# A fused RetNet and RWKV channel-mix kernel: v scaled on GpSimd in ten blocks, five differences moved, half-array transposes from block 3, and a new order of pieces

## The chip, the cores and the metric

The kernel runs on one core of a Trainium2 chip. The metric is the device time of one execution in microseconds. The core has five instruction queues that run side by side, each in its own order: TensorE (PE, with its weight loads PEld), VectorE (DVE), ScalarE (ACT), GpSimd (POOL) and SyncE (SP). SP, ACT and POOL issue DMAs. A wait is a semaphore ahead of an instruction; everything behind it in the same queue waits too.

## The reference

Two layers, one after the other, in float32. The first is a linear recurrence with a decay per head, the second a mixture of each token with the one before it, and two matrix products.

```python
# q, k, v: (B, H, S, D) = (4, 8, 768, 64)
for t in range(S):
    state = gamma[h] * state + outer(k[t], v[t])
    y[t]  = q[t] @ state / sqrt(D)
x = y.transpose(0, 2, 1, 3).reshape(B, S, 512)
x_prev = x shifted by one token, zero at each sequence's start
xk = mu_k * x + (1 - mu_k) * x_prev
xr = mu_r * x + (1 - mu_r) * x_prev
k2 = relu(xk @ w_k) ** 2            # w_k: 512 x 1024
out = sigmoid(xr @ w_r) * (k2 @ w_v)  # w_r: 512 x 512, w_v: 1024 x 512
```

## The kernel before

The 4 x 768 tokens are cut into twelve blocks of 256 tokens, three to a sequence. A block goes through two stages: attention in a chunked form, with a state carried between the blocks of a sequence, then the channel mix. There is no scheduler. The constant `ORDER` (lines 24 to 75) is a list of some 630 words; a loop at the end of the kernel reads them one by one and records the instructions of each, so the order of the words is the order in each engine's queue. A word is a piece, its block and its parts; `~v ~a ~p ~s` says which engine does it (VectorE, ScalarE, GpSimd, SP), and `@67` which PSUM banks it takes. So `vs.3~p` is block 3's scaling of v on GpSimd, and `K.0.2@1` is the key product of block 0, part 2, into bank 1.

The words, with the helper and its line in the kernel before:

- `lq lk lv` load q, k, v of a block (L232 in two halves of 64 columns a token, L237 in one); `wk wr wv` load weights (L725, L728, L732), always on POOL. Loads by POOL convert q and k to float16 on the way; those by SP do not, and `ck cq` convert after them (L245).
- `vs` scales v by powers of the decay (L255): 128x1024 float32 times a broadcast constant, result in float16.
- `Tq Tk` transpose q and k on TensorE. A "whole" block takes 16 matmuls over the full height of the array (L274); otherwise 32 matmuls of 64x64, on the two halves of the height (L280). `Eq Ek` copy the result out of PSUM (L243).
- `S` scores (L320, L333, L341), `M` their causal mask on VectorE (L349, L356), `C` the blocks' states (L368, L386, L397), `U` their running sum (L421), `G` its decay to the next block (L426 on ScalarE, L430 on VectorE), `I Y J` the products with the carried state and with the masked scores (L443, L464, L480, L491).
- `D` writes the result, times the factor gy, into the tile xT (L509, L516); `gy` builds that factor (L708 to L718).
- `dx` takes the difference of each token to the one before it (L531), `X.n.w.j` the mixture (L560): xk for w = 0, xr for w = 1, in four parts j. Both read two tiles in SBUF.
- `K` the key product (L574 for two blocks together, L584 for one), `Qa Qb` its ReLU and square on ScalarE (L593, L601, L605), `R` the gate product (L614), `s` its sigmoid (L620), `V` the value product (L626), `O` the product of both (L632), `st` the store on SP (L639). `Vc Oc sc` are the last 128 tokens in two column halves (L644, L651, L656).
- `z` is a filler: matmuls on zeros that nothing reads (L693 in float32, L700 in float16).

Blocks 3 and 4, 6 and 7, 9 and 10 share their K pieces. Raw loads of q, k and v go through rings of four tiles, the scaled v (`vs`) and the transposed q and k through rings of three. DMAs take their semaphores from two rings of eight, one for those issued by POOL and one for those issued by SP and ACT; each waits until the one eight places before it in its ring has landed.

What the change touches besides the order are the sets that choose the form of a block:

```python
WHOLE = (0, 1, 2, 3, 4, 5)     # L21
WIDE = (2, 3, 4)               # L22
def whole(n):                  # L208
    return n in WHOLE or n in WIDE
```

Of the kernel before, what the change touches and what calls it, by code (L numbers as in the profile page):

```python
# [36 lines left out]
R.1.1@7 X.2.0.1 vs.3~p M.3.0~v Ek.4~a K.2.3@1 Qa.2.3 K.2.0@6 Qa.2.0 M.3.1~v S.4.1@45 M.4.1~v
Tq.5@1 Eq.5~a C.3@23 U.3.0~v U.3.1 s.1.1 vs.4~v R.1.0@6 s.1.0 G.3~a K.2.1@0 I.3@45 Qb.2.3 S.4.0@23
M.4.0~v Y.3 C.4@67 U.4.0 U.4.1 G.4~a K.2.2@1 Qb.1.1 I.4@23 J.3 Qa.2.1 Qa.2.2 Y.4 Qb.2.0 D.3~v
V.0.0.0@6 Tq.6@45 J.4 dx.3~v V.1.1.0@7 D.4~v dx.4~v X.3.0.1 V.0.1.0@0 V.1.0.0@1 X.2.1.2 Qb.2.2  # L40
wv.1~p V.0.0.1 Eq.6~a V.0.1.1 lq.7~p lk.6~p Tk.6@45 Ek.6~a O.0.0 Tq.7@23 Eq.7~a V.1.0.1 S.6@45
lk.5~p Tk.5@6 X.3.0.2 X.3.0.3 X.3.0.0 K.3.3@2 Qb.2.1 K.3.2@3 O.1.0 Ek.5~a O.0.1 X.3.1.1 M.6~v
lv.5~p vs.5~v K.3.5@0 Qa.3.5 Qa.3.3 K.3.4@6 V.1.1.1 Qa.3.2 lv.6~p C.5@01 S.5@45 Qa.3.4 vs.6~v
C.6@23 Qb.3.3 Qb.3.2 O.1.1 M.5~v U.5.0 X.2.1.3 U.5.1 U.6.0~a U.6.1 U.6.2 U.5.2 U.6.3 K.3.0@6
X.2.1.1 Qa.3.0 Qb.3.0 V.2.0.0@7 K.3.6@4 Qa.3.6 K.3.7@6 st.0.1 Qa.3.7 Qb.3.7 I.5@01 I.6@45 V.2.0.1
K.3.1@3 Qa.3.1 Qb.3.1 X.2.1.0 R.2.0@6 lk.8~p Tk.8@23 lv.7~p Y.5 X.3.1.0 vs.7~v X.3.1.3 Y.6 X.3.1.2
s.2.0 R.3.1@6 D.5~v dx.5~v st.1.1 st.0.0 Ek.8~a X.5.0.3 O.2.0 X.5.0.0 V.2.1.0@2 X.5.0.1 R.3.0@3
D.6~v G.6~a Qb.3.4 s.3.0 s.3.1 lv.8~p R.2.1@0 s.2.1 X.5.1.3 X.5.0.2 R.4.0@1 s.4.0 V.2.1.1 lk.7~p
# [30 lines left out]
def kernel(  # L79
# [180 lines left out]
    def turned(n, a, j0):  # L260
        if whole(n):
            return banks("T", n, a, j0).bitcast(F16).rearrange("c (j i p) -> c j i p", j=NJ, i=2)
        pt = banks("T", n, a, j0).bitcast(F16)[:, :, 0 : 2 * NJ * D]
        return pt.rearrange("c u (j i p) -> c u j i p", j=NJ, i=2)

    def trans(a):
        def go(e, n, j0=0, j1=NJ):
            pt = turned(n, a, j0)
            src = (K16 if a else Q16)(n)
            for j in range(j0, j1):  # L270
                for i in range(2):
                    if whole(n):
                        for s, h, jo, hp in heads(j):
                            nc.tensor.transpose(  # L274
                                pt[low(s), j, i, :], src[:, h, i * D : i * D + D], ident
                            )
                        continue
                    for u in range(2):
                        for s, h, jo, hp in heads(j):
                            nc.tensor.transpose(  # L280
                                pt[low(s), u, j, i, :], src[low(u), h, i * D : i * D + D],
                                ident[low(u), low(u)],
                            )
# [506 lines left out]
```

## Time and profile before

| What | Value |
|---|---|
| Median of 3 runs | 156.21 us (155.82 to 156.54) |
| Span of the profiled execution, first to last instruction | 154.9 us |
| TensorE busy | 146.0 us, 2423 matmuls |
| VectorE busy | 126.9 us, 205 instructions |
| ScalarE busy | 99.4 us |
| GpSimd busy (DMA issues included) | 55.5 us, 65 instructions |
| DMA | 22.31 MB in 45768 packets |
| HBM read, written | 24.31 MB, 6.29 MB |

The span is one profiled execution; its time in the manner of the runs is not listed, and the median of the runs stands 1.3 us above the span. Busy shares of TensorE are not utilisation, since its matmuls overlap: what a group costs is read from the start of one to the start of the next. VectorE's instructions overlap by some 0.08 us, so they too are read from start to start. "Landing" is the time from a DMA's issue to its last byte.

### The profile page before, as it was taken

To read this page: it belongs to the slowest core of one execution; us is meant where nothing else is said; L and a number is where in the kernel's file an instruction comes from. 1 tells how busy PE (TensorE), PEld (TensorE's weight loads), DVE (VectorE), ACT (ScalarE), POOL (GpSimd) and SP (SyncE) were. 2 spreads that over 40 slices of the span, in tenths; PEclk is the share of its full clock that TensorE was granted. 3 is DMA by queue.
4 is the path that set the end of the run, shared out by engine and by line. 5 is a ranking of instruction groups with operands and counts; after the bars stand their busy time and mean duration, and the time that the engine had idled before them with its cause. 6 is when DMAs were issued, how large, how long until landed. Compare 5 with 4: busy or idle time off the path is not lost.

```text
span 154.9 us, 5520 instructions
## 1 busy us (share of the span) xinstructions
PE 146.0 (94%) x2423; PEld 83.9 (54%) x2423; DVE 126.9 (82%) x205; ACT 99.4 (64%) x186; POOL 55.5 (36%) x65
## 2 busy tenths in 40 slices
...
DVE  2588999999899999999999999998999998110541
...
PEclk9999999999999999999999999999999999999999
DMA  5999999999999999996999510025000023101254
GB/s 144 263 219 194 197 228 171 196 241 218 156 180 212 199 241 258 223 234 181 116 147 204 150 68 4 4 74 203 4 4 0 6 82 136 52 0 72 96 209 169
DMA packets 45768, 22.31 MB, mean 144 GB/s; under 512 B 37416, under 2 KB 41392, under 8 KB 45744
## 3 DMA queue, kind: packets, MB, share of 16 engines
...
HBM read 24.31 MB, written 6.29 MB: 198 GB/s over the span
## 4 chain that ended last, share of the span: by engine, by line
PE 55%; DVE 24%; DMA 12%; issue 4%; POOL 3%; DVEq 0%; POOLq 0%
PE ps L626 19%; DMA v<-in_v_dram 12%; PE ps L614 9%; PE ps L574 9%; PE ps L584 8%; DVE a L356 3%; DVE xk L560 3%; DVE xr L560 3%; DVE vs L255 3%; DVE dx L531 2%; DVE xT L516 2%; DVE tg L421 2%; DVE os L632 2%; PE ps L443 2%; DVE a L349 1%
## 5 line engine op out<-in xcount | busy, mean ns | idle before, releaser
L626 PE MATMUL ps<-wv,k2s 128*128 128x512 f16 x184 | 43.4, 379 | 0.0
L593 ACT ACTIVATE kr<-ps 128x512 f32<-128x512 f32 x48 | 27.8, 596 | 23.1 <-PE ps L574 18.0
L626 PEld LDWEIGHTS <-k2s 128*128 128x128 f16 x184 | 17.4, 98 | 20.0
L632 DVE SCALAR_TENSOR_TENSOR os<-ps,rs 128x512 f32<-128x512 f32 x23 | 15.4, 683 | 14.5 <-ACT rs L620 7.4
L614 PE MATMUL ps<-wr,xr 128*128 128x512 f16 x96 | 24.1, 380 | 0.0
L584 PE MATMUL ps<-xk,wk 128*128 128x256 f16 x192 | 24.0, 273 | 0.0
L232 POOL DMA_DIRECT2D k<-in_k_dram x20 | 17.7, 898 | 15.2 <-PE ps L280 10.5
L574 PE MATMUL ps<-xk,wk 128*128 128x512 f16 x96 | 22.5, 379 | 0.0
L584 PEld LDWEIGHTS <-wk 128*128 128x128 f16 x192 | 18.1, 98 | 4.9 <-DMA wk<-in_moe_w_k_dram 0.6
L620 ACT ACTIVATE rs<-ps 128x512 f32<-128x512 f32 x24 | 13.7, 594 | 9.3 <-PE ps L614 8.9
L560 DVE SCALAR_TENSOR_TENSOR xr<-dx,mu,xT 128x256 f16<-128x256 f32 (+1 forms) x36 | 19.2, 564 | 0.1
L560 DVE SCALAR_TENSOR_TENSOR xk<-dx,mu,xT 128x256 f16<-128x256 f32 (+1 forms) x36 | 18.8, 567 | 0.2
L232 POOL DMA_DIRECT2D v<-in_v_dram x18 | 16.2, 915 | 1.4 <-DMA q<-in_q_dram 0.5
L243 ACT COPY kT<-ps 128x1024 f16<-128x1024 f16 (+1 forms) x13 | 12.2, 947 | 5.2 <-PE ps L280 4.1
L601 ACT ACTIVATE k2s<-kr 128x512 f16<-128x512 f32 x24 | 14.9, 628 | 0.3
L574 PEld LDWEIGHTS <-wk 128*128 128x128 f16 x96 | 9.2, 98 | 10.8
L531 DVE TENSOR_TENSOR dx<-xT 128x1024 f32<-128x1024 f32 x12 | 14.6, 1223 | 0.3
L605 ACT ACTIVATE k2s<-kr 128x512 f16<-128x512 f32 x24 | 14.5, 628 | 0.1
L243 ACT COPY qT<-ps 128x1024 f16<-128x1024 f16 (+1 forms) x13 | 12.3, 949 | 2.4 <-PE ps L274 2.2
L614 PEld LDWEIGHTS <-xr 128*128 128x128 f16 x96 | 8.8, 97 | 9.2 <-DVE xr L560 0.2
L255 DVE TENSOR_TENSOR vs<-v,csm_sb 128x1024 f16<-128x1024 f32 x10 | 12.1, 1216 | 2.0 <-DMA v<-in_v_dram 2.0
L356 DVE TENSOR_TENSOR a<-ps,c_sb 128x1024 f16<-128x1024 f32 (+1 forms) x12 | 12.2, 1040 | 0.5 <-PE ps L333 0.4
...
## 6 DMA issues: line engine op xcount, KB each, us to landing
out_dram<-os SPq DMA_DIRECT2D x23, 256.0 KB, 2.2
v<-in_v_dram POOLq DMA_DIRECT2D x18, 256.0 KB, 8.3
q<-in_q_dram POOLq DMA_DIRECT2D x11, 256.0 KB, 8.2
...
wk<-in_moe_w_k_dram POOLq DMA_DIRECT2D x2, 512.0 KB, 11.0
...
```

The costliest lines, as they stand in the source:

```text
L232: e.dma_start(out=dst[:, :, i * D : i * D + D], in_=src[:, i * P : i * P + P].rearrange("h p d -> p h d"),)
L243: e.copy(out=out, in_=in_)
L255: e.tensor_tensor(out=VS(n), in0=V32(n).rearrange("p h (i d) -> p i h d", i=2), in1=gks[:, int(half(n) or wide(n)), :, :, None].to_broadca ...
L356: nc.vector.tensor_tensor(out=a_full(n)[:, i, :, j0:j1], in0=pairs(banks("S", n, i, j0))[:, :, j0:j1], in1=(below if wide(n) else causal[: ...
L531: e.tensor_tensor(out=DX(k)[:, :, m * TM + t0 : m * TM + t1], in0=x[:, :, c + t0 : c + t1], in1=x[:, :, c - 1 + t0 : c - 1 + t1], op=ALU.s ...
L560: nc.vector.scalar_tensor_tensor(out=XM[w](k)[:, j, t0:t1], in0=DX(k)[:, j, t0:t1], scalar=mu[:, w * NCO + j : w * NCO + j + 1], in1=x[:, ...
L574: nc.tensor.matmul(banks("K", n, g), lhsT=wk16[:, co, g * P : g * P + P], rhs=XM[0](k)[:, co, :], start=(co == 0), stop=(co == NCO - 1),)
L584: nc.tensor.matmul(pz[:, i, :], lhsT=wk16[:, co, fo * P : fo * P + P], rhs=XM[0](k)[:, co, m * TM + t0 : m * TM + t1], start=(i == 0 and c ...
L593: nc.scalar.activation(out=kr, in_=banks("K", n, g, *u), func=AF.Relu)
L614: nc.tensor.matmul(banks("R", n, tb), lhsT=XM[1](k)[:, co, t : t + P], rhs=wr16[:, co, :], start=(co == 0), stop=(co == NCO - 1),)
L626: nc.tensor.matmul(banks("V", n, tb), lhsT=K2(n)[:, fo, tb * P : tb * P + P], rhs=wv16[:, fo, :], start=(fo == 0), stop=(fo == NFO - 1),)
L632: nc.vector.scalar_tensor_tensor(out=OS(2 * n + tb), in0=banks("V", n, tb), scalar=1.0 / (KSC * KSC), in1=RS(2 * n + tb), op0=ALU.mult, op ...
```

## The change

The sets become

```diff
-WHOLE = (0, 1, 2, 3, 4, 5)
+WHOLE = (0, 1, 2)
 WIDE = (2, 3, 4)
@@ def whole(n):
-        return n in WHOLE or n in WIDE
+        return n in WHOLE
```

so blocks 3, 4 and 5 are transposed in the 64x64 form as well. The rest is a new `ORDER`. Its head, with the old one's, and the later words that matter here:

```diff
-lq.0.0.2~s gy.0 lv.0~p lk.0.0.2~s ck.0.0.2~v mu lk.0.2.4~p lq.0.2.4~p gy.1~a lv.1~p lk.1~p lq.1~p
-cq.0.0.2~v lq.2~p wk.0~p z.12@6 Tk.0.0.2@0 Tq.0.0.2@1 Ek.0.0.2~a Eq.0.0.2~a mt@2 wk.1~p vs.0~v
-z.2@6 S.0.0.0.2@01 me M.0.0.0.2~v S.0.1.0.2@45 Tk.0.2.4@2 M.0.1.0.2~v Tq.0.2.4@3 lk.2~p C.0@67
-U.0.0~v Ek.0.2.4~a Eq.0.2.4~a z.1@0 S.0.0.2.4@23 M.0.0.2.4~v I.0@45 S.0.1.2.4@01 M.0.1.2.4~v z.1@2
-Y.0 U.0.1 G.0~a vs.1~p Tk.1@7 Ek.1~a D.0~v dx.0~v lv.2~p lq.3~p lk.3~p C.1@01 U.1.0 X.0.0.0
-X.0.0.3 Tq.1@6 Eq.1~a z.4@2 S.1.1@67 lq.4~p X.0.0.2 I.1@45 Tq.2@0 M.1.1~v S.1.0@23 Eq.2~a wr~p
-X.0.0.1 z.1@7 K.0.0@6 M.1.0~v U.1.1 G.1~a lk.4~p Qa.0.0 X.0.1.0 X.0.1.1 Qb.0.0 Y.1 D.1~v dx.1~v
...
+lk.0.2.4~p gy.0~v lk.0.0.2~s lv.0~p mu~a ck.0.0.2~v z.12@6 Tk.0.0.2@0 lq.0.0.2~s cq.0.0.2~a
+Tq.0.0.2@1 lq.0.2.4~p Eq.0.0.2~a z.2@2 Tk.0.2.4@1 mt@2 me~a Ek.0.0.2~a z.2@3 S.0.1.0.2@23 gy.1~v
+vs.0~v S.0.0.0.2@45 M.0.0.0.2~v Ek.0.2.4~a z.1@6 Tq.0.2.4@1 C.0@67 U.0.0~a U.0.1~v lk.1~p Tk.1@0
+Eq.0.2.4~a I.0@67 S.0.0.2.4@45 lv.1~p lq.1~p Ek.1~a M.0.1.0.2~v lq.2~p M.0.0.2.4~v S.0.1.2.4@23
+M.0.1.2.4~v lk.2~p wk.1~p z.3@1 Y.0 Tq.1@2 vs.1~p C.1@45 G.0~a D.0~v Eq.1~a z.2@1 S.1.1@67 S.1.0@23
+U.1.0~v I.1@01 U.1.1~v G.1~a Tq.2@5 wk.0~p Eq.2~a M.1.0~v M.1.1~v dx.0~p X.0.0.3~v X.0.0.1~v lv.2~s
+Tk.2@4 Ek.2~a lk.3~p z.4@2 z.1@2 S.2.0@67 wr~p X.0.0.2~v X.0.0.0~v Y.1 D.1~v dx.1~v lq.3~p X.1.0.1~v
+X.1.0.0~v X.1.0.2~v X.1.0.3~v S.2.1@45 M.2.1~v M.2.0~v X.1.1.3~v K.0.2@2 K.0.3@3 Qa.0.3~a K.0.0@0
...
+lv.3~s R.0.1@3 lv.4~p s.0.1~a Qb.0.1~a X.1.1.1~v X.1.1.0~v R.1.0@7 Tk.4@45 Ek.4~a R.1.1@6 s.1.1~a
...
+K.2.1@2 Qb.1.2~a S.4.0@45 S.4.1@01 wv.1~p lk.5~p vs.3~p C.3@67 U.3.0~a M.4.0~v U.3.1~v vs.4~p G.3~v
...
+U.4.0~v lk.7~p V.1.1.0@2 I.4@01 J.3 V.0.0.0@6 D.3~v dx.3~p U.4.1~v V.0.0.1 O.0.0~v st.0.0~s Y.4
...
```

On each engine this gives:

- `vs` is on GpSimd in blocks 1, 2, 3, 4, 5, 6, 8, 9, 10 and 11 (before: 1 and 3); blocks 0 and 7 stay on VectorE.
- `dx` is on GpSimd in blocks 0, 3, 7, 8 and 9 (before: none).
- The second part of gy goes from ScalarE to VectorE, as do the decays of blocks 3, 6, 9 and 10; the cast of the first half of q and three state copies are on ScalarE.
- v is loaded on SP in blocks 2, 3, 5, 6, 9, 10 and 11 (before: 11), the others on POOL. On SP the loads of v.2 and v.3 follow those of the first halves of k.0 and q.0; v.2's two DMAs carry no wait, v.3's wait for the landing of the first constant and of the first half of k.0.
- POOL's queue begins k.0 (second half), v.0, q.0 (second half), k.1, v.1, q.1, q.2, k.2, wk.1, vs.1, wk.0, dx.0, k.3, wr, q.3, k.4, vs.2, q.4, v.4, wv.0, wv.1, k.5, vs.3, vs.4, k.7, dx.3, q.5, vs.5, q.7, k.6, q.6, vs.6.
- The fillers are 11 matmuls in float16 and those of z.12 and z.4 (before: 6 and the same two).

More of the change, by code (lines that the diff above doesn't have):

```diff
@@ L37 @@
[L37 to L48, printed above, removed]
@@ new lines @@
+U.1.0~v I.1@01 U.1.1~v G.1~a Tq.2@5 wk.0~p Eq.2~a M.1.0~v M.1.1~v dx.0~p X.0.0.3~v X.0.0.1~v lv.2~s
+Tk.2@4 Ek.2~a lk.3~p z.4@2 z.1@2 S.2.0@67 wr~p X.0.0.2~v X.0.0.0~v Y.1 D.1~v dx.1~v lq.3~p X.1.0.1~v
+X.1.0.0~v X.1.0.2~v X.1.0.3~v S.2.1@45 M.2.1~v M.2.0~v X.1.1.3~v K.0.2@2 K.0.3@3 Qa.0.3~a K.0.0@0
+Qa.0.0~a Qb.0.0~a Qa.0.2~a X.1.1.2~v K.0.1@3 K.1.3@0 K.1.2@1 Qb.0.3~a Qa.1.3~a K.1.0@2 Qb.1.3~a
+Qa.1.2~a lk.4~p vs.2~p C.2@6 K.1.1@7 U.2.0~v I.2@01 X.0.1.0~v Qa.1.0~a Qb.1.0~a Tk.3@45 Qb.0.2~a
+Ek.3~a Y.2 Qa.0.1~a X.0.1.1~v X.0.1.3~v X.0.1.2~v R.0.0@6 s.0.0~a lq.4~p Qa.1.1~a Tq.3@45 Eq.3~a J.2
@@ new lines @@
+lv.3~s R.0.1@3 lv.4~p s.0.1~a Qb.0.1~a X.1.1.1~v X.1.1.0~v R.1.0@7 Tk.4@45 Ek.4~a R.1.1@6 s.1.1~a
+D.2~v dx.2~v X.2.0.0~v X.2.0.2~v wv.0~p X.2.0.1~v X.2.0.3~v S.3.1@23 M.3.1~v Qb.1.1~a S.3.0@01
+X.2.1.0~v M.3.0~v s.1.0~a X.2.1.1~v Tq.4@45 Eq.4~a K.2.3@6 Qa.2.3~a K.2.0@7 Qa.2.0~a Qb.2.0~a
+K.2.1@2 Qb.1.2~a S.4.0@45 S.4.1@01 wv.1~p lk.5~p vs.3~p C.3@67 U.3.0~a M.4.0~v U.3.1~v vs.4~p G.3~v
+K.2.2@3 Qa.2.2~a I.3@45 Y.3 X.2.1.3~v C.4@67 lv.5~s Qa.2.1~a Qb.2.1~a X.2.1.2~v R.2.0@3 M.4.1~v
+U.4.0~v lk.7~p V.1.1.0@2 I.4@01 J.3 V.0.0.0@6 D.3~v dx.3~p U.4.1~v V.0.0.1 O.0.0~v st.0.0~s Y.4
@@ new lines @@
+Tk.5@45 J.4 V.2.0.0@6 D.4~v dx.4~v X.3.0.0~v V.0.1.0@7 V.0.1.1 Qb.2.2~a O.0.1~v st.0.1~s s.2.0~a
+Qb.2.3~a V.2.0.1 O.2.0~v Ek.5~a X.3.1.2~v G.4~a X.3.0.1~v lq.5~p R.2.1@3 s.2.1~a V.1.1.1 V.1.0.0@3
+Tq.5@67 Eq.5~a Tk.7@45 Ek.7~a X.3.0.2~v vs.5~p C.5@01 V.1.0.1 X.3.1.0~v X.3.0.3~v K.3.5@6 K.3.2@7
+O.1.0~v lv.6~s Qa.3.5~a Qb.3.5~a K.3.1@6 U.5.0~v O.1.1~v U.5.1~v U.5.2~v I.5@01 lq.7~p S.5@23
+Tq.7@45 X.3.1.1~v Qa.3.2~a lk.6~p Qa.3.1~a K.3.3@6 Qa.3.3~a X.3.1.3~v K.3.6@7 Qa.3.6~a Eq.7~a
+Qb.3.6~a M.5~v lq.6~p Y.5 D.5~v dx.5~v X.5.0.0~v X.5.0.2~v vs.6~p Tk.6@23 Ek.6~a V.2.1.0@7 V.2.1.1
@@ new lines @@
+Tq.6@01 Eq.6~a Qb.3.3~a X.5.0.1~v C.6@45 X.5.0.3~v S.7@23 K.3.0@6 K.3.7@0 U.6.0~a Qa.3.0~a Qb.3.0~a
+st.2.0~s st.1.0~s lk.8~p R.4.0@1 s.4.0~a M.7~v O.2.1~v lq.9~p K.5.0@6 U.6.1~v U.6.2~v Qa.5.0~a
+lv.7~p lq.8~p U.6.3~v Qa.3.7~a lv.8~p Qb.3.1~a vs.7~v X.5.1.3~v R.4.1@1 s.4.1~a st.1.1~s I.6@67
+Tk.8@23 Ek.8~a S.6@45 M.6~v R.3.0@0 s.3.0~a K.3.4@1 C.7@23 G.6~v lq.11~p lk.10~p X.5.1.0~v Qa.3.4~a
+Tq.8@45 Qb.3.2~a Qb.3.4~a Y.6 U.7.0~v lv.9~s U.7.1~v X.5.1.1~v K.5.3@1 D.6~v U.7.2~v V.3.0.0@0
+U.7.3~v dx.6~v Qa.5.3~a lq.10~p Qb.3.7~a V.3.0.1 K.5.1@1 I.7@23 Eq.8~a S.8@45 M.8~v Tk.10@67
@@ new lines @@
+Qb.5.3~a Qa.5.1~a Ek.10~a O.3.0~v V.4.0.0@1 vs.8~p V.4.0.1 lk.9~p C.8@45 Y.7 X.5.1.2~v G.7~a U.8.0~v
+Tq.9@67 Eq.9~a U.8.1~v st.2.1~s st.3.0~s D.7~v V.4.1.0@0 V.4.1.1 O.4.1~v O.4.0~v U.8.2~v R.3.1@6
+s.3.1~a R.5.0@2 s.5.0~a st.4.1~s V.3.1.0@6 I.8@23 Tk.9@45 dx.7~p X.6.0.3~v X.6.1.2~v X.6.0.2~v
+Ek.9~a X.6.1.0~v Tq.10@01 Eq.10~a X.6.0.1~v V.3.1.1 K.5.2@7 lv.10~s X.6.0.0~v Qb.5.1~a vs.9~p C.9@45
+Y.8 U.9.0~v Qa.5.2~a Qb.5.2~a Tq.11@01 Eq.11~a Qb.5.0~a O.3.1~v vs.10~p K.6.4@7 U.9.1~v Qa.6.4~a
+st.4.0~s lv.11~s K.6.3@6 vs.11~p K.6.6@0 U.9.2~v U.9.3~v K.6.7@7 D.8~v I.9@23 Qa.6.6~a Qa.6.3~a
@@ new lines @@
+C.10@01 Qb.6.3~a X.6.1.1~v G.9~v dx.8~p S.9@45 M.9~v K.6.0@6 st.3.1~s U.10.0~v U.10.1~v Qa.6.7~a
+X.8.1.1~v X.8.0.1~v U.10.2~v X.8.0.0~v X.6.1.3~v U.10.3~v X.8.0.2~v K.6.1@7 G.10~v Qb.6.6~a Qa.6.1~a
+Qb.6.1~a K.6.2@4 lk.11~p Qa.6.2~a V.5.0.0@7 K.6.5@0 Qa.6.5~a V.5.0.1 Qb.6.2~a X.8.1.2~v R.5.1@0
+s.5.1~a Qa.6.0~a O.5.0~v Qb.6.7~a Qb.6.4~a V.5.1.0@1 V.5.1.1 X.8.0.3~v O.5.1~v st.5.1~s st.5.0~s
+Qb.6.0~a Qb.6.5~a I.10@67 S.10@45 M.10~v Y.9 D.9~v R.7.0@1 R.6.0@0 s.6.0~a s.7.0~a Y.10 Tk.11@45
+C.11@23 U.11.0~v U.11.1~v Ek.11~a U.11.2~v K.8.2@0 D.10~v dx.9~p dx.10~v X.9.0.1~v X.9.0.3~v
@@ new lines @@
+V.6.0.0@1 R.7.1@2 s.7.1~a K.8.1@4 Qa.8.1~a K.8.0@2 Qa.8.0~a S.11@45 M.11~v X.9.0.2~v I.11@67 V.6.0.1
+V.7.0.0@2 K.8.3@3 Qa.8.3~a V.7.0.1 X.9.0.0~v X.9.1.2~v K.9.0@3 K.9.1@4 Qa.9.1~a Qb.8.3~a Y.11
+X.8.1.0~v X.9.1.0~v X.8.1.3~v D.11~v Qb.8.0~a R.6.1@5 V.7.1.0@4 dx.11~v K.9.2@6 Qa.9.0~a s.6.1~a
+Qa.8.2~a Qb.8.2~a X.11.0.3~v X.11.1.1~v X.11.0.0~v X.11.0.2~v V.7.1.1 K.9.3@0 Qa.9.3~a R.8.0@5
+Qb.8.1~a V.6.1.0@0 V.6.1.1 K.9.5@3 K.9.7@7 Qa.9.5~a Qb.9.1~a X.9.1.3~v O.6.0~v O.7.1~v X.9.1.1~v
+R.10.1@3 V.8.1.0@4 Qb.9.3~a Qa.9.2~a Qb.9.2~a st.6.0~s Qb.9.5~a O.6.1~v st.6.1~s V.8.1.1 K.9.4@6
```

39 lines of the change are left out of this document (8 added, 31 removed).

## The prediction

> **What bounds the kernel now.** I read the page first (busy shares, the slices), then the busy times by stage, then the chain, then single rows of the timelines and the DMA issues. The page:
>
> ```profile
> PE 146.0 (94%) x2423; PEld 83.9 (54%) x2423; DVE 126.9 (82%) x205; ACT 99.4 (64%) x186; POOL 55.5 (36%) x65
> ...
> DVE  2588999999899999999999999998999998110541
> ...
> PEclk9999999999999999999999999999999999999999
> DMA  5999999999999999996999510025000023101254
> ```
>
> VectorE and the DMA engines are full until about 75 us (slice 19), TensorE to the end. By stage (columns: stretch, then its length, then busy time of PE, PEld, DVE, ACT, POOL, clock, DMA, GB/s):
>
> ```profile
> 20.00:44.00 24.00, 23.02 (x395) 16.71 (x385) 22.65 (x35) 19.55 (x37) 16.48 (x19) 1.00 1.51 203
> 44.00:75.00 31.00, 30.87 (x622) 16.42 (x618) 30.24 (x47) 22.96 (x43) 16.88 (x21) 1.00 1.42 207
> 75.00:115.00 40.00, 39.87 (x896) 22.96 (x895) 38.22 (x60) 29.34 (x57) 6.10 (x7) 1.00 0.59 95
> ```
>
> VectorE leads until 75 us, TensorE from then on; the chain says so too (pieces of v, vs and DVE work first, only PE pieces from 75.1 us). Its head and tail, and three rows of TensorE's timeline:
>
> ```profile
> 1.26 6.88 DMA v<-in_v_dram
> 8.16 0.45 DVE vs L255
> ...
> 150.42 0.89 PE ps L644 x8
> 151.33 0.42 DVE os L651
> ```
> ```profile
> 13.85 0.64 PE L274 MATMUL ps<-c_sb,q 128*64 128x128 f16 x16
> 14.41 1.12 PE L693 MATMUL ps<-zero 128*128 128x512 f32 x2
> ...
> 18.42 1.10 PE L584 MATMUL ps<-xk,wk 128*128 128x256 f16 x8
> ...
> 50.29 0.45 PE L280 MATMUL ps<-c_sb,k 64*64 64x64 f16 x32
> 50.57 0.44 PE L280 MATMUL ps<-c_sb,q 64*64 64x64 f16 x32
> ```
>
> Since matmuls overlap, I price a group by start to start. A V, R or joint K group is 0.863 us, a single K 0.875 (0.109 x 8), and each change from attention groups to these costs 0.1 more (0.957 to 0.967 instead of 0.863). Behind the first K (18.42 us) stand 103.9 us of K, R, V and Vc, 21.0 of attention groups and fillers and 52 changes: an end at 148.5 us; the last matmul ends at 151.3. The missing 2.8 us are VectorE's: from the end of X.0.0.2 (17.0 us) its own instructions, start to start (X 0.40, joint X 0.66, mask 1.135, sum 0.35, difference 1.2, D 1.26 or 1.43, O 0.61), add up to 58.2 us at the last sum that I.7 needs, and 73.3 + 1.9 us of TensorE stand behind I.7: 150.4 us. Two segments, VectorE then TensorE, thus give the end but for 0.9 us of slips. I use the same sum for the change. 3.6 us lie behind the last matmul (151.3 to 154.9), the same in both; the profiled span is 1.3 us under the median of 156.2 us.
>
> **Transposes.** Blocks 3 to 5 take the 64x64 form: 0.28 us for 32 (50.29 to 50.57) against 0.56 for 16 (13.85 to 14.41). Six groups: -1.7 us of TensorE. The 96 more instructions are inside that. Five more 16-bit fillers (226 ns each) stand before the first K, hidden in head waits.
>
> **VectorE.** Eight more scalings of v go to GpSimd (8 x 1.135 = 9.1 us) and five differences (5 x 1.2 = 6.0); the last step of gy, four decays and a few copies change sides (about +1). Its sum falls from 125.8 to 111.8 us. On GpSimd a scaling took:
>
> ```profile
> L255 DVE TENSOR_TENSOR vs<-v,csm_sb x10: 1212/1214/1225, 8.2 to 103.8; 128x1024 f16<-128x1024 f32 x10
> L255 POOL TENSOR_TENSOR vs<-v,csm_sb x2: 1897/1918/1939, 11.0 to 37.0; 128x1024 f16<-128x1024 f32 x2
> ```
>
> Ten scalings and five differences are 28.8 us there at 1.92 each; no row has a difference on GpSimd, its bounds are 1.2 (VectorE's) and 2 x 1.92, and I take the scaling's since elements and inputs are as many.
>
> **The head.** Here I expect the loss. The order of the changed kernel puts v.2 and v.3 on SP. SP has nothing to wait for ahead of them: v.2's two halves follow the first two loads at once, v.3's wait only for the constants' and k.0's landing (3.1 and 4.0 us before). In before, v.2 was issued at 12.9 us and v.3 at 24.8. So 1 MB enters ahead of v.1. Does that delay POOL's loads? DMA issues in three stretches (last column: us to landing; 54.0 to 54.3, 64.5 to 66, 87 to 90 us):
>
> ```profile
> v<-in_v_dram POOLq DMA_DIRECT2D x1, 256.0 KB, 7.8
> out_dram<-os SPq DMA_DIRECT2D x1, 256.0 KB, 6.8
> ```
> ```profile
> v<-in_v_dram SPq DMA_DIRECT2D x2, 256.0 KB, 6.4
> ```
> ```profile
> out_dram<-os SPq DMA_DIRECT2D x2, 256.0 KB, 2.0
> ```
>
> A store takes 2.0 us on idle engines and 6.8 behind POOL's loads: what is issued first lands first, whichever queue. Halves of v land 1.13 us apart in before (23.2, 24.4), so four cost 4.5 us. In before v.1 and k.1 had both landed by 12.3 us; now v.1, behind k.1, lands at 12.3 + 4.5 = 16.8. Then: vs.1 on GpSimd 1.92, C.1 0.45, two sums 0.7, two masks 2.3, four X 1.6: first X set at 23.8 (18.5 before, the end of X.0.0.1). TensorE's own words between C.1 and the first K take 5.9 us: 24.6. q.1, q.2, k.2 and the first wk (1.45, 1.44, 1.9, 2.55 by their spacing) land by 24.1; the other half of wk is issued only behind vs.1 in POOL's queue and lands at 26.6 (20.3 before). K.0.0 needs it. Behind K.0.0 stand 119.2 us and 48 changes, 4.8: 150.6, and with the tail **154.2 us**. Nothing hides the late loads: all three engines wait for the same ones. Later loads gain as much as these lose, but TensorE has nothing left to save there.
>
> From the first X set VectorE needs 9.1 us to X.0.1.2, and 112.9 + 4.4 us of TensorE follow R.0.0: 23.8 + 126.4 = 150.2. The same sum is 149.3 at K.2.3, 148.8 at I.4, 147.4 at K.3.5, 144.6 at K.6.4. So VectorE is no longer the limit, by 0.4 us at first and by 6 later: 14 us less work, bought after the place where time was lost.
>
> **What is queued behind GpSimd's new waits.** POOL issues loads in order: q.5 stands behind dx.3, which waits for D.3; q.7, k.6 and q.6 behind vs.5. With TensorE dense, dx.3 ends near 50.7 us, q.5 lands near 56 (4.3 to 6.2 us from issue to landing after a pause, rows of 73 to 76 us) and Tq.5 wants it at 56.6. These slips can cost nothing or 2 us; I take 0.7, near the 0.9 that the sum missed in before. GpSimd's products may also hold VectorE, nothing to 1.92 us each. No row decides it: both products of before ran beside masks, which read PSUM. Only vs.2 falls where VectorE has under half a microsecond to spare; I take half, 1.0. Sum: 154.2 + 1.7 = 155.9 us, 1.0 over the span before, so 157.2 as a median.
>
> The Trainium skill (SBUF — State Buffer, Who interferes with whom) says that a VectorE instruction with two SBUF inputs and a GpSimd instruction that reads SBUF exclude each other for the whole instruction, and that whichever started first keeps the port. No run here shows it yet; by it X, differences and scalings would all be held, which is the second rival below.
>
> **Rivals.** *The head is not delayed* (faster): SP's loads ride beside POOL's. For it: the stages show DMA shares of 1.4 to 1.5, so the engines work on several transfers at once. Against it: the landings in issue order. Then v.1 lands at 12.3, the second wk at 22.1, the end is 22.1 + 124.0 + 3.6 + 1.7 = 151.4, time 152.7.
>
> *GpSimd holds VectorE* (slower): eight products stand before K.6.4, where 6.0 us are spare; from 0.75 us a product this decides. At half of 1.92 each the end moves by 1.7 us, at all of it by 9.4; with 3.1 it is 154.2 + 0.7 + 3.1 = 158.0, time 159.3. For it: X, dx and vs are about 40% of VectorE's remaining work, and one cast of 128x512 took 628 ns, its twin 406. Against it: X took 468 to 480 ns beside POOL's DMA issues throughout, and some products will fall on masks.
>
> *A slow clock in the head*: in before TensorE never waited over 0.9 us between its matmuls and PEclk is full throughout. Now it waits some 2 us each for q.0 and k.1. If the clock dropped for 3.4 us of K groups, half of that, 1.7, is lost: 157.6, time 158.9. The Trainium skill (TensorE: Matmul & The Clock Gate, What's actually happening) has the clock halved after an idle window of about 3.4 us; these waits are shorter, by my sum, so the chance is small.
>
> **Numbers.** The forecast has 0.44 (its own range 155.6 to 158.6), the free head 0.24, the holds 0.24, the clock 0.08. About 0.5% (0.8 us) can be told from no change. Faster: 0.22 of the free head and 0.06 of the forecast's low end. Same: 0.20 and 0.02. Slower: 0.18 of the forecast, 0.24, 0.08. The range goes from a free head with fewer slips, 152.3, to holds a little above the price, 160.5.
>
> **What would show it.** Right: vs.1 waits for v.1 until about 17 us, the first K starts near 24 to 25 (18.4 before), and from there TensorE is dense: DVE's row falls below 9 in many slices, L280 has 576 matmuls. Wrong if the first K starts before 21 us, if X's mean rises above 0.55 us, if Tq.5 or Tk.6 waits over 2 us for a load, or if PEclk shows less than 9.

## The result

The changed kernel takes 183.42 us (181.93 to 186.36, four runs) against 156.11 (155.82 to 156.54) beside it: a ratio of 1.172, 95% interval 1.164 to 1.181, 27 us slower. The run of 186.36 us counts as slow, and the ratio uses the other three. Its profiled execution took 184.6 us, span 182.8. The prediction (157.2 us, 152.3 to 160.5) had the likelier sign and 1.0 us of a loss of 27.

The page of the changed kernel, the lines that answer to the first ones of the prediction:

```profile
PE 156.2 (85%) x2524; PEld 87.1 (48%) x2524; DVE 125.7 (69%) x194; ACT 96.3 (53%) x169; POOL 71.5 (39%) x66
...
DVE  3262799979886999095972899997778892250232
...
PEclk9995899999699999699957999699999999999999
DMA  5999999999554799899991159171300003033063
```

DVE is below 9 in most slices, as foreseen, but TensorE isn't full in its place (the stages below). VectorE has 11 instructions fewer and is still busy for 125.7 us. PEclk falls below 9 in seven slices where it was 9 throughout. The same stages as before (stretch, length, PE, PEld, DVE, ACT, POOL, clock, DMA, GB/s):

```profile
20.00:44.00 24.00, 19.78 (x413) 13.31 (x397) 22.13 (x28) 17.43 (x30) 18.12 (x17) 1.00 1.50 196
44.00:75.00 31.00, 25.90 (x401) 14.40 (x402) 25.72 (x36) 12.87 (x24) 11.67 (x11) 0.93 0.95 124
75.00:115.00 40.00, 33.68 (x850) 19.14 (x848) 29.78 (x44) 24.52 (x40) 22.52 (x20) 0.88 0.94 137
```

The chain of waits in order of time (start, length, what), cut to five pieces that are not TensorE's work. In before's chain the last load lands at 36.8 us, and one product on GpSimd and VectorE's and TensorE's work stand behind it.

```profile
3.79 10.36 DMA k<-in_k_dram
...
24.38 13.43 DMA q<-in_q_dram
...
65.10 8.92 DMA v<-in_v_dram
...
90.09 2.21 issue
...
111.59 2.39 DVE xk L565
```

To place the loss I add to each word's start on TensorE the start-to-start prices of all that stands behind it. The end so projected is 144.1 us at the first word (145.1 in before: the transposes' gain, less the new fillers) and 178.0 at the last wait, K.9.0; in before it goes from 145.1 to 149.4. So 33.9 us of waits stand against 4.3. By these prices, and so as estimates, they come at: the head to K.0.0, 9.6; K.2.3 to S.4.0, 5.5; V.1.0.0, 1.0; K.3.3 and Y.5, 3.8; Tq.8, 2.1; K.5.3 to K.5.1, 5.2; V.4.1.0, 0.7; K.6.4 to K.6.7, 3.9; K.9.0, 2.1.

### The profile page after: what moved, and what is told of

Read it like the earlier page. It is cut to its first block, busy times and chain, and to the rows that moved or that the text cites. A ratio compares the mean times of both kernels' runs of the same rounds, so it can differ in the third digit from the quotient of the medians.

```text
span 182.8 us, 5712 instructions
## 1 busy us (share of the span) xinstructions
PE 156.2 (85%) x2524; PEld 87.1 (48%) x2524; DVE 125.7 (69%) x194; ACT 96.3 (53%) x169; POOL 71.5 (39%) x66
## 4 chain that ended last, share of the span: by engine, by line
PE 33%; DMA 23%; issue 19%; POOL 10%; DVE 10%; POOLq 2%; SPq 1%; DVEq 0%
PE ps L631 12%; DMA v<-in_v_dram 9%; DMA q<-in_q_dram 7%; PE ps L619 6%; DMA k<-in_k_dram 6%; PE ps L579 4%; PE ps L589 4%; POOL dx L536 3%; POOL k L237 3%; DVE xk L565 2%; PE ps L285 2%; POOLq L790 2%; POOL vs L260 1%; DMA out_dram<-os 1%; DVE dx L536 1%
## 5 line engine op out<-in xcount | busy, mean ns | idle before, releaser
L631 PE MATMUL ps<-wv,k2s 128*128 128x512 f16 x184 | 45.7, 390 | 1.1 <-ACT rs L625 1.1
L589 PE MATMUL ps<-xk,wk 128*128 128x256 f16 x192 | 26.4, 291 | 4.8 <-DVE xk L565 4.2
L579 PE MATMUL ps<-xk,wk 128*128 128x512 f16 x96 | 25.8, 415 | 3.4 <-DVE xk L565 3.4
L260 POOL TENSOR_TENSOR vs<-v,csm_sb 128x1024 f16<-128x1024 f32 x10 | 20.0, 2001 | 20.5 <-DMA v<-in_v_dram 17.2
L565 DVE SCALAR_TENSOR_TENSOR xk<-dx,mu,xT 128x256 f16<-128x256 f32 (+1 forms) x36 | 25.0, 734 | 2.0 <-POOL dx L536 1.8
L625 ACT ACTIVATE rs<-ps 128x512 f32<-128x512 f32 x24 | 14.3, 598 | 20.8 <-PE ps L619 11.5
L589 PEld LDWEIGHTS <-wk 128*128 128x128 f16 x192 | 19.5, 104 | 10.9 <-DVE xk L565 2.8
L536 POOL TENSOR_TENSOR dx<-xT 128x1024 f32<-128x1024 f32 x5 | 10.5, 2096 | 31.3 <-DVE xT L514 26.3
L565 DVE SCALAR_TENSOR_TENSOR xr<-dx,mu,xT 128x256 f16<-128x256 f32 (+1 forms) x36 | 21.9, 638 | 0.0
L579 PEld LDWEIGHTS <-wk 128*128 128x128 f16 x96 | 9.6, 104 | 15.9 <-DVE xk L565 4.0
L514 DVE TENSOR_TENSOR xT<-ps,gy_sb 128x512 f32<-128x512 f32 x14 | 9.6, 689 | 6.7 <-PE ps L448 6.0
```

Of the source, the lines that this page charges most:

```text
L260: e.tensor_tensor(out=VS(n), in0=V32(n).rearrange("p h (i d) -> p i h d", i=2), in1=gks[:, int(half(n) or wide(n)), :, :, None].to_broadca ...
L536: e.tensor_tensor(out=DX(k)[:, :, m * TM + t0 : m * TM + t1], in0=x[:, :, c + t0 : c + t1], in1=x[:, :, c - 1 + t0 : c - 1 + t1], op=ALU.s ...
L565: nc.vector.scalar_tensor_tensor(out=XM[w](k)[:, j, t0:t1], in0=DX(k)[:, j, t0:t1], scalar=mu[:, w * NCO + j : w * NCO + j + 1], in1=x[:, ...
L579: nc.tensor.matmul(banks("K", n, g), lhsT=wk16[:, co, g * P : g * P + P], rhs=XM[0](k)[:, co, :], start=(co == 0), stop=(co == NCO - 1),)
L589: nc.tensor.matmul(pz[:, i, :], lhsT=wk16[:, co, fo * P : fo * P + P], rhs=XM[0](k)[:, co, m * TM + t0 : m * TM + t1], start=(i == 0 and c ...
L631: nc.tensor.matmul(banks("V", n, tb), lhsT=K2(n)[:, fo, tb * P : tb * P + P], rhs=wv16[:, fo, :], start=(fo == 0), stop=(fo == NFO - 1),)
```

## The theories

- **Head**: 1 MB of v on SyncE ahead of v.1, and later v loads behind stores.
- **Holds**: GpSimd's products and differences hold VectorE's instructions with two inputs from SBUF.
- **Clock**: each idle time of TensorE over 2 us costs a window of half clock besides.
- **Stops**: TensorE waits for its own instructions.
- **Order**: the list of pieces is late by itself.

Most kernels ran once. The three runs of the changed kernel that the ratio uses lie 2.7 us apart, so I read a difference between two single runs only from about 3 us on, and rest the finer points on traces.

## Experiments: first round

**e1, the products back.** In the changed kernel, the eight `vs` and five `dx` that moved go back to VectorE:

```diff
-dx.0~p vs.2~p vs.4~p dx.3~p vs.5~p vs.6~p vs.8~p dx.7~p vs.9~p vs.10~p vs.11~p dx.8~p dx.9~p
+dx.0~v vs.2~v vs.4~v dx.3~v vs.5~v vs.6~v vs.8~v dx.7~v vs.9~v vs.10~v vs.11~v dx.8~v dx.9~v
```

> The changed kernel with the eight scalings and five differences put back on VectorE, order and loads otherwise as changed. Theory A (GpSimd's products hold VectorE's two-input instructions; TensorE waits for those, and the clock drops behind such waits): X goes back to 0.48 and 0.74 us, dx to 1.22, the first K starts at 25 to 27 us, the 2.7 us wait before K.2.3 is gone, and although VectorE has 15 us more to do the time falls to 163 to 170 us. Theory B (the head's loads and the late loads of v make the loss, the holds are hidden): the time stays at 178 us or more, since VectorE has more work and the loads are the same. Theory C (instruction fetches stop TensorE): the two idle times of 2.2 us inside transpose groups stay, 176 to 182.

Measured: 181.49 us. The holds go (X 479 and 746 ns, as in before), the loss stays. TensorE now waits for the products instead, at C.5 (2.6 us), C.6 (2.6) and C.9 (2.9). The row puts 1.6 us down to a copy by ScalarE, but that wait is C.6's, and C.6 begins 0.05 us after its product ends:

```profile
L373 PE MATMUL ps<-vs,k 64*64 64x64 f16 x200 | 3.1, 196 | 7.9 <-DVE vs L260 6.3 <-ACT k2s L606 1.6
```

**e2, v on SyncE alone.** In before:

```diff
-lv.2~p ... lv.3~p
+lv.2~s ... lv.3~s
```

> The kernel before with one edit: v.2 and v.3 are loaded by SP. Theory B (what is issued first lands first): v.1 lands at 14 to 16 us instead of 10.9, the scaling of block 1 and all behind it move by 4 us, time 159 to 162. Rival (SP's loads ride beside POOL's): v.1 lands by 12 us, time 155 to 157.

Measured: 164.41 us, 8.2 more than before. The first K starts at 25.80 us for 18.42, v.1 lands at 13.8 for 10.8, q.1 at 20.0, and the clock is halved from 9.0 to 26.1 us. This is above what either theory gave: the edit alone costs nearly a third of the whole loss.

**e3, ten products on GpSimd alone.** In before, the eight more `vs` on GpSimd, the order unchanged:

```diff
-vs.2~v vs.4~v vs.5~v vs.6~v vs.8~v vs.9~v vs.10~v vs.11~v
+vs.2~p vs.4~p vs.5~p vs.6~p vs.8~p vs.9~p vs.10~p vs.11~p
```

> The kernel before with one edit: v is scaled on GpSimd in the same ten blocks as in the change, at the old places. Theory A: X and dx that overlap a scaling take up to 1.9 us more, eight holds of about 1 to 1.5 us for 9.1 us of work taken off VectorE; with the clock dropping behind waits 158 to 170 us. Rival (VectorE is relieved at no cost): X stays at 0.48, VectorE's sum falls by 9 us and the time to 150 to 153.

Measured: 167.68 us, 11.5 more. Groups of instructions (line, engine, operation, tiles and shape, count | busy us, mean ns of one | idle before): the rows have means of 1223, 478 and 475 ns in before.

```profile
L531 DVE TENSOR_TENSOR dx<-xT 128x1024 f32<-128x1024 f32 x12 | 17.4, 1454 | 0.3
L560 DVE SCALAR_TENSOR_TENSOR xk<-dx,mu,xT 128x256 f16<-128x256 f32 x24 | 15.8, 698 | 0.1
L560 DVE SCALAR_TENSOR_TENSOR xr<-dx,mu,xT 128x256 f16<-128x256 f32 x24 | 12.4, 546 | 0.0
```

The excess is 12 x 0.23 + 24 x 0.22 + 24 x 0.07 = 9.8 us, as much as the eight products took from VectorE (9.1 by the prediction's price). VectorE is busy for 128.1 us, not less than before. And held pieces are ones that TensorE waits for: K.1.1 and K.2.3 wait 2.0 and 2.2 us for an X. But the longest wait has another cause. R.3.1 waits 3.2 us, and 3.4 us of half clock follow; together they are about 5 of the 11.5 us, by my estimate. The two loads of v.7 stand in GpSimd's queue behind products that themselves wait for v (6.3 and 4.1 us); they are issued only at about 66 us, and vs.7 on VectorE, with the X behind it, comes late:

```profile
73.75 1.23 DVE L255 TENSOR_TENSOR vs<-v,csm_sb 128x1024 f16<-128x1024 f32 x1 [4.04 <-DMA v<-in_v_dram]
```

**e4, whole transposes in blocks 0 to 5.** In the changed kernel:

```diff
-WHOLE = (0, 1, 2)
+WHOLE = (0, 1, 2, 3, 4, 5)
-Tk.3@45 Tq.3@45 Tk.4@45 Tq.4@45 Tk.5@45 Tq.5@67
+Tk.3@4 Tq.3@4 Tk.4@4 Tq.4@4 Tk.5@4 Tq.5@6
```

> The changed kernel with the full-height transposes kept in blocks 3 to 5 (16 matmuls in one PSUM bank instead of 32 in two). Theory C (the extra instructions make TensorE wait for its instruction fetch): the idle times of 2.2 us inside transpose and score groups at 71 and 90 us go, the clock keeps full there, 174 to 179 us. Rivals A and B: six groups of 0.28 us more on TensorE, the same waits, 182 to 186 us.

Measured: 178.74 us, 4.7 less although TensorE has 1.7 us more to do. One stop stays (2.59 us, ending at 75.7). The one that ended at 92.3 is gone, but a new one of 1.48 us ends at 107.5: those over 0.3 us add up to 4.5 us for 4.9. So the gain isn't that of fewer stops; K.2.3 waits 1.0 us for 2.7, and the half clock of 6.8 us from 91.4 us on is gone.

## Experiments: the head, the clock, the late loads

**f1, v.2 and v.3 on GpSimd.** In the changed kernel (f2 and f3 include this):

```diff
-lv.2~s ... lv.3~s
+lv.2~p ... lv.3~p
```

> The kernel after with the loads of v.2 and v.3 issued by GpSimd instead of SyncE, at the same places of the order; everything else as after (183.4 us). Theory A (the 1 MB of v that SyncE enters early holds up v.1, q.2, wk.1 and wk.0, and TensorE's waits for them halve its clock): v.1 lands near 11 us instead of 15.7, the first K starts near 20 to 23 us instead of 27.1, no stretch at half clock before 20 us, and 176 to 179 us. Theory B (the head of this order is late whatever queue v.2 and v.3 use): the first K stays at 25 us or later, the half clock in the head stays, 181 to 185 us.

Measured: 175.77 us, 7.7 less than the median (6.2 to 8.8 less than the three runs). The first K starts at 21.25 us (27.12), the half clock in the head is gone. DMA issues of the first 30 us (last column: median us to landing), first of the changed kernel, then of f1:

```profile
v<-in_v_dram SPq DMA_DIRECT2D x6, 256.0 KB, 12.5
...
q<-in_q_dram POOLq DMA_DIRECT2D x4, 256.0 KB, 13.2
```
```profile
q<-in_q_dram POOLq DMA_DIRECT2D x4, 256.0 KB, 8.0
```

GpSimd's q loads land 5.2 us sooner. The head theory holds, in both orders: it costs 8.2 us when added to before and 7.7 when taken from the changed kernel.

**f2, every later v on GpSimd too.**

```diff
-lv.5~s lv.6~s lv.9~s lv.10~s lv.11~s
+lv.5~p lv.6~p lv.9~p lv.10~p lv.11~p
```

> As the run before it, and the later v loads (5, 6, 9, 10, 11) are issued by GpSimd too, so that none waits on SyncE behind a store. Theory A (late v is what the products and so C.5 to C.9 wait for): 'vs <- DMA' falls from 17.2 us to under 5, and 168 to 174 us, 4 us or more under the run with the head alone. Theory B (it is the order: VectorE gives the shifts X too late): the wait for v goes, but TensorE's waits for X stay, within 2 us of the run with the head alone. Rival C: the loads now stand behind GpSimd's waiting products and differences, and come later still: above the run with the head alone.

Measured: 177.9 us, not less than f1. That v.6 comes late (issued behind a store at 64.7 us, its product waiting 9.0 us in the changed kernel) is real, but taking it away doesn't help: K.6.4 alone then waits 4.1 us. The two runs also differ in their stops (10.8 us for 8.8 in f1, those over 0.3 us), by about as much as in their times.

**f3, and the products back.** f2 with the edit of e1.

> All v loads on GpSimd, and the eight products and five differences that the change moved back on VectorE: what is left of the change is the order of the pieces and the 64x64 transposes. If loads and products together carry the 27 us (A and D): 158 to 164 us, and the half-clock stretches are gone. If the order itself is late (B): 170 us or more, with TensorE waiting on VectorE's products and shifts and two or more stretches at half clock.

Measured: 179.82 us. With head, late loads and holds out of it, the order still costs 23 us: 2.6 us each at C.5 and C.6, 1.1 at C.8, 2.9 at C.9, all for products on VectorE, and 2.5 us of a stop at 84 us. (Another stop, of 1.6 us, lies inside C.6's wait.)

**f4, fillers in the changed kernel.**

```diff
-Tq.0.2.4@1 ... Tk.1@0 ... K.2.3@6 ... K.6.4@7
+z.8@1 Tq.0.2.4@1 ... z.8@0 Tk.1@0 ... z.12@6 K.2.3@6 ... z.8@7 K.6.4@7
```

> The kernel after with four added filler words on TensorE, just ahead of four of its waits (8 ahead of the transposes Tq.0.2.4 and Tk.1 in the head, 12 ahead of K.2.3, 8 ahead of K.6.4): 36 more in all, about 8 us of TensorE work at full clock that lies in idle time. Theory C (an idle time of over 2 us costs a further 1.7 us of clock per window): the half-clock stretches at 12.9 to 19.7, 47.0 to 50.4 and 115.3 to 118.7 go, the mean clock rises from 0.935 to 0.96 or more, and the time falls by 2 to 5 us to 178 to 181. If the clock costs nothing (the waits set the time anyway): 183 to 187 us, no gain or a loss by the work added.

Measured: 184.67 us. The mean clock rises from 0.935 to 0.981 and the time does not fall. The fillers set K.0.0 back from 29.6 to 32.7 us, and that is regained behind K.2.3, so this run alone doesn't price the clock. The next two do.

**f5, e2 with fillers in its head.**

```diff
-mt@2 Tk.0.2.4@2 Tq.0.2.4@3 Tk.1@7 Tq.1@6 S.1.1@67
+z.4@2 mt@2 z.4@2 Tk.0.2.4@2 z.4@3 Tq.0.2.4@3 z.4@7 Tk.1@7 z.8@6 Tq.1@6 z.8@7 S.1.1@67
```

> The kernel before with v.2 and v.3 on SyncE (164.4 us against 156.2 when it ran alone, 17 us of the head at half clock), and 32 fillers more (8 us of TensorE work at full clock) ahead of six of the waits in the head. It parts the clock from the late loads. Theory C (a good part of that 8 us is the clock): the half clock from 9.0 to 26.1 us shrinks to 3.4 us or less and the time falls to 159.5 to 162.5. If the late loads alone make the loss: the clock is restored, and the time stays at 163.5 to 166.

Measured: 164.57 us against e2's 164.41. Its clock, the first line of this page that differs:

```profile
PEclk9999999999999999999999999999999999999999
```

17 us at half clock were worth nothing: the first K starts at 25.33 for 25.80, since loads and VectorE set it. In the head the clock theory falls.

## Experiments: the stops, one window of clock, the transposes alone

**g2, f1 with whole transposes in blocks 6 to 11** (3 to 5 stay 64x64):

```diff
-WHOLE = (0, 1, 2)
+WHOLE = (0, 1, 2, 6, 7, 8, 9, 10, 11)
```

with one bank for two in each of their twelve words.

> The kernel after with v.2 and v.3 on GpSimd (175.8 us), and blocks 6 to 11 in the whole form of the transposes: 384 instructions of TensorE and as many weight loads fewer less half, so 16 for 32 in each of 12 words, for 12 x 0.28 = 3.4 us of matmul time more. If TensorE's two stops of 2.9 us come from too many short instructions close together (a 16 KB fetch of instructions that comes too late): both stops shrink below 1 us or go, with the half-clock window behind one of them, 170 to 175 us. If they come at the same places whatever the count, 177 to 181 us.

Measured: 171.06 us, 4.7 less than f1 with 3.4 us more of transposes. What goes is this. TensorE's timeline in the changed kernel (start, length, what, in brackets the idle time ahead and what ended it), then the DMA queues from 70.5 to 73.5 us:

```profile
73.44 0.34 PE L285 MATMUL ps<-c_sb,q 64*64 64x64 f16 x18 [2.27 <-issue]
...
92.30 0.64 PE L469 MATMUL ps<-a,vs 64*64 64x64 f16 x30 [2.21 <-issue]
```
```profile
q8 instruction: 1, 0.02, 2.0%
```

TensorE stops in the middle of a word, with 14 of 32 transposes done, and waits for no semaphore. The stop lasts from 71.17 to 73.44 us; a 16 KB transfer of the instruction queue begins at 71.09 us, as the work runs out, and takes 1.0 us. In f1 the same two stops, 8 us earlier and at the same instructions, are 2.81 and 2.91 us long. In before 19 such transfers begin too, each ahead of need: no idle time of TensorE over 0.6 us stands at one after 20 us.

What such a stop is shows when TensorE's records (its matmuls and weight loads) are numbered in order of start. In all 16 traces, every idle time over 0.3 us that waits for no semaphore stands at record 193 or 194 plus a multiple of 256; the two above are at 1986 and 2754, three times 256 apart, and so are those of f1. The 19 transfers for 5057 records fit 256 instructions each. Work goes on 2.2 to 2.9 us after a transfer begins, well behind its end. So TensorE waits for the next 256 instructions wherever less work than that is left when their transfer begins. The idle times of this kind over 0.3 us add up to 0.3 us in before, 4.9 in the changed kernel, 8.8 in f1 and 2.6 in g2.

Behind 25 us, g2 has two of 0.80 and 0.28 us (one of 1.4 us at 22 us, in f1 too, stays), and the clock is full:

```profile
PE 149.9 (89%) x2332; PEld 85.7 (51%) x2332; DVE 122.2 (72%) x194; ACT 96.6 (57%) x169; POOL 74.3 (44%) x70
...
PEclk9999999999999999999999999999999999999999
```

**g3, f1 with one filler word.**

```diff
-K.6.4@7
+z.12@7 K.6.4@7
```

> The kernel after with v.2 and v.3 on GpSimd (175.8 us), and one filler word of 12 ahead of K.6.4, where TensorE stands 2.5 us for a shift and the clock then halves for 3.4 us. Theory C: the half-clock stretch at 105 to 108.4 us goes, the end comes 1.2 to 1.7 us earlier, 174.0 to 174.8 us, and the words from K.6.4 to K.6.7 start 0.863 apart instead of 1.7. If VectorE's shifts set the pace of these words anyway: the clock is full, the end is unchanged within 0.5 us.

Measured: 178.28 us. The clock at K.6.4 is full: the 16 matmuls of K.6.4, K.6.3, K.6.6 and K.6.7 take 3.62 us for 5.31. But VectorE's mask is next: K.6.2 waits 1.26 us for it, and from K.6.4 to K.9.0 it is 27.76 us against 28.00 in f1. Of 1.7 us restored, 0.24 reach K.9.0. The whole run is 2.5 us slower than f1 for other reasons: K.9.0 waits 0.6 us longer, and at the end VectorE's last output pieces wait 4.9 us for a store to land (3.0 in f1).

**g4, 64x64 transposes of blocks 3 and 4 alone.** In before, in two banks:

```diff
-Tq.3@3 ... Tk.3@0 ... Tq.4@1 ... Tk.4@0
+Tq.3@23 ... Tk.3@03 ... Tq.4@13 ... Tk.4@01
```

and `WHOLE = (0, 1, 2, 5)`. With these banks the values of blocks 3 and 4 are not the reference's; only the time is used.

> The kernel before with the 64x64 transposes in blocks 3 and 4 alone, in two PSUM banks each: step b of the prediction for four of its six groups. By the prediction's price 4 x 0.28 = 1.1 us less TensorE work and 64 instructions more. If the price holds to the end: 155.0 to 155.5 us (ratio 0.993 to 0.996), the fastest of all. If VectorE sets the end of that stage, as the prediction has it until 75 us, or the second bank adds waits: 156 to 157.5 us, no gain. If 64x64 transposes bring TensorE to a stop for instructions: a stop of over 1 us before 60 us and 158 us or more.

Measured: 160.34 us, ratio 1.028 (1.023 to 1.033). No stop for instructions; from 27.9 to 38 us Tq.3, K.1.0, S.3.0, S.3.1 and R.1.1 start 0.6 to 1.1 us late each, 4.0 in all, behind banks that are still being copied out. So the run doesn't price the transposes alone: the second bank hides what they save. A placing of blocks 3 to 5 that costs no bank waits was not found.

## Experiments: what is left

**h1, g2 with products and differences back** (the edit of e1), and **h2, g2 with the five `dx` back**:

```diff
-dx.0~p dx.3~p dx.7~p dx.8~p dx.9~p
+dx.0~v dx.3~v dx.7~v dx.8~v dx.9~v
```

> The kernel after with v.2 and v.3 on GpSimd and the whole transposes in blocks 6 to 11 (171.1 us, no stop and a full clock), and now the eight products and five differences of the change back on VectorE: the order of the pieces alone, with head, instruction stops and products taken out. 3.4 us of it are the longer transposes. If GpSimd's holds carry the rest (12 us over the kernel before): 160 to 165 us. If the order is late by itself, because it places the products just ahead of the chunk words C that need them: 168 to 174 us, with TensorE waiting for VectorE's products at C.5, C.6, C.8 and C.9, about 9 us in all.

> As the run before it, but only the five differences go back to VectorE; the eight products stay on GpSimd. VectorE has 6 us more of its own work and 10 us less beside which it is held. If the differences are what makes the shifts late (K.0.3, S.4.1, K.6.4, K.9.0 wait, 5.9 us together): 166 to 169 us. If it is the products: 170 to 173 us, the waits stay.

Measured: h1 177.62 us, h2 171.4, g2 171.06. With only vs.1 and vs.3 left on GpSimd the order is 6.5 us slower: it places each product just ahead of the C that needs it, and C.5, C.6 and C.9 wait 1.9 to 2.4 us for VectorE. So this order needs GpSimd's products, and pays for them in holds. h2 has 3.0 us of idle TensorE behind 55 us for g2's 7.7, as the theory of the differences had it, and pays that back at one place, where a product meets an X. VectorE and GpSimd in h2:

```profile
45.79 4.12 DVE L565 SCALAR_TENSOR_TENSOR xr<-dx,mu,xT 128x256 f16<-128x256 f32 x2
```
```profile
47.69 1.93 POOL L260 TENSOR_TENSOR vs<-v,csm_sb 128x1024 f16<-128x1024 f32 x1
```

Two X take 4.12 us for 0.88, and TensorE stands 3.0 us for them. The excess, 3.2 us, is more than the product's 1.9: the second X started at 46.19 us, 1.5 us ahead of the product, beside DMA issues of GpSimd.

## Why the prediction was wrong, step by step

**What bounds the kernel, and the two-segment sum**: right for before, wrong as a form for the change. The sum took TensorE as dense behind K.0.0 once VectorE had 14 us less to do. It is not a sum of busy time that decides in this order but single waits: of 33.9 us of TensorE's waits, 24.3 stand behind K.0.0 (in before all its waits are 4.3). This is the step that failed most. "TensorE is dense from there" was a condition, and the text gave no price for its failing; slack computed at five words (0.4 to 6 us) was slack against VectorE's undisturbed sum.

**The head**: that early loads of v on SyncE set GpSimd's loads back was right, and the size was too small. v.1 landed at 15.7 us (16.8 foreseen), but the first K started at 27.12, not 24.6, and K.0.0 waited for wk until 29.64, not 26.6. "What is issued first lands first, whichever queue" failed, and v.1's time came out near by luck. In the changed kernel a half of v.3, issued on SyncE at 3.03 us, landed at 17.56, behind v.1, which GpSimd issued at 4.67 and which landed at 15.74. Before's own rows were against the rule too: a store issued at 58.68 us landed at 63.59, ahead of a load of k issued at 58.29 (65.23). The four q loads of GpSimd took 13.2 us to land instead of f1's 8.0 while 1.5 MB of v went through SyncE (v.5 follows v.2 and v.3; the step priced 1 MB). So loads of two queues that are on their way together share the engines. The sum priced the head at 4.5 us (155.9 against the free head's 151.4); the runs show 7.7 and 8.2.

**VectorE's 15.1 us saved**: did not happen. Busy time fell by 1.2 us (126.9 to 125.7). The holds took the rest:

```profile
L565 DVE SCALAR_TENSOR_TENSOR xk<-dx,mu,xT 128x256 f16<-128x256 f32 x24 | 13.5, 606 | 0.1
L536 DVE TENSOR_TENSOR dx<-xT 128x1024 f32<-128x1024 f32 x7 | 12.7, 1807 | 0.2
...
L565 DVE SCALAR_TENSOR_TENSOR xk<-dx,mu,xT 128x512 f16<-128x512 f32 x12 | 11.5, 989 | 1.8 <-POOL dx L536 1.8
L565 DVE SCALAR_TENSOR_TENSOR xr<-dx,mu,xT 128x512 f16<-128x512 f32 x12 | 10.6, 890 | 0.0
```

Against before's means (478, 1223, 745, 742 ns; xr in the small form 475, here 512) that is 24 x 0.13 + 7 x 0.58 + 12 x 0.24 + 12 x 0.15 + 24 x 0.04 = 12.8 us. The sum had 1.0; the second rival had 3.1, with 9.4 as its end. Its condition, 0.75 us a product, is met: 12.8 over 15 is 0.85. Its mechanism was right. Its price was not: it set eight products against 6 us of slack, and the slack was gone with the first waits. And 0.85 is only an average: the 12.8 us fall on nine instructions, eight of them beside seven products and one difference (0.6 to 2.1 us each), the ninth (an X at 23.86 us, 1.5 us longer) beside GpSimd's DMA issues alone. Rows of both engines side by side, VectorE first:

```profile
39.78 3.33 DVE L536 TENSOR_TENSOR dx<-xT 128x1024 f32<-128x1024 f32 x1
43.15 2.00 DVE L565 SCALAR_TENSOR_TENSOR xk<-dx,mu,xT 128x256 f16<-128x256 f32 x1
```
```profile
40.10 1.92 POOL L260 TENSOR_TENSOR vs<-v,csm_sb 128x1024 f16<-128x1024 f32 x1
42.64 2.23 POOL L260 TENSOR_TENSOR vs<-v,csm_sb 128x1024 f16<-128x1024 f32 x1 [0.62 <-PE ps L285]
```

The difference is longer by 2.1 us, a whole product; the X by 1.5. The Trainium skill (SBUF — State Buffer, Who interferes with whom) says that the two exclude each other for the whole instruction; the lengths agree. It says that the first to issue keeps the port; the difference that starts 0.3 us before the product is the one that is longer. In the records it is VectorE's instruction that gets longer, whichever starts first, so the start in the records doesn't tell who keeps it; GpSimd's products keep a mean of 2.00 us for 1.92. Masks, sums and D, with an operand in PSUM, keep their means beside GpSimd (1.22 us for a mask), as the prediction assumed.

**Transposes, -1.7 us**: the time of a word was right (0.28 for 0.56), the sign of the edit not shown. e4 and g2 both gain 4.7 us by the longer form in this order, but only in g2 do the stops shrink (8.8 to 2.6 us); in e4 they stay (4.9 to 4.5) and other waits get shorter. The sentence "the 96 more instructions are inside that" failed: a long stop for instructions costs 2.2 to 2.9 us here, and none was among the rivals. The Trainium skill (Runtime: NRT & Kernel Launch, Instruction fetch mechanics) has fetches of 16 KB that are mostly hidden. Before's trace agrees; the changed kernel's, with stops of 2.27 and 2.21 us, does not.

**Slips behind GpSimd's waits, 0.7**: Tq.5 cost nothing measurable; the late one was v.6 on SyncE, behind a store that waits for O, a queue that the step did not walk. vs.6 waited 9.0 us for it, and its price is not separate: f2 took that wait away and gained nothing. Behind vs.6, GpSimd issues the load of v.7 only at 78.7 us; VectorE waits 1.8 us for it, and the wait of 2.1 us at Tq.8 follows.

**The slow clock, +1.7 at a chance of 0.08**: it came, five times, 23.9 us in all (3.4 or 6.8 us each), in the profile's own stretches of half clock. The chance was small because the waits were to be shorter than the window of 3.4 us that the Trainium skill (TensorE: Matmul & The Clock Gate, What's actually happening) names; the stretches are multiples of that length, but waits of 1.8 to 2.7 us were enough. The stretches start at 12.89, 47.02, 74.33, 91.40 and 115.29 us, whole steps of 3.41 us apart, and in the step just ahead of each TensorE was idle for 2.1 to 2.5 us. So where a wait falls counts too: f1's stop of 2.81 us lies across two steps (1.7 and 1.1 us idle), and no half clock follows. By f5 (0 of 17 us) and g3 (0.24 of 1.7) it is a symptom: where another engine sets the next wait, the half clock is spent in time that is lost anyway.

**The tail, 3.6 us in both**: 1.0 us too small. The changed kernel's last matmul ends at 178.2 us of 182.8, since VectorE's last output pieces wait 3.0 us for a store to land (in before such a wait there is 0.3 us):

```profile
178.02 0.69 DVE L637 SCALAR_TENSOR_TENSOR os<-ps,rs 128x512 f32<-128x512 f32 x1 [3.01 <-DMA out_dram<-os]
```

**The account.** By single runs in a row: head 7.7 us (183.4 to 175.8), stops with the clock behind them 8.1 (f1 to g2: 4.7, and, by price, the 3.4 us of longer transposes that g2 carries), and 11.5 over before that remain when those 3.4 us are taken off g2. These 11.5 are holds and order together. In g2's trace five waits of TensorE, 1.1 to 1.7 us each and 6.4 together, show how: S.4.1, K.6.4 and K.6.2 stand behind X that products or a difference held for 1.4 to 1.7 us; Tq.8 stands behind a mask after vs.7, whose load came late; K.9.0 stands behind a difference that GpSimd itself does. With only two products left on GpSimd (h1) the order is late by more. e3 has eight more products in the other order at 11.5 us, of which about 5 are the late load behind GpSimd's own waits. How much of them a third order could give back, is open. Why the fetches of instructions start late in this order and not in before, is open too; what the stop is, is shown. No version here beats the kernel before.
